# Strassen-like second layer of a fused attention and channel-mixer kernel: seven products summed in held PSUM banks for groups 1 to 5

## The chip, the cores and the metric

The kernel runs on one core of a Trainium2 chip. The metric is the device time of one execution in microseconds; lower is better. The engines are named as in the profile: PE (TensorE matmuls), PEld (TensorE weight loads), DVE (VectorE), ACT (ScalarE), POOL (GpSimd) and SP (SyncE, which issues DMAs).

## The reference

Causal attention with a bias from a running sum of `max(s, 0)`, on 8 batches of 8 heads, 576 positions, 64 dimensions; its output, as 8 x 576 tokens of 512 features, goes through a low-rank mixer over the positions and then a two-layer mixer over the features:

```
bias = -(cum[:, :, :, None] - cum[:, :, None, :])          # cum = cumsum(max(s, 0))
scores = where(causal, -1e9, q @ k.T / 8 + minimum(bias, 0))
x = softmax(scores) @ v                                    # to (8, 576, 512)
u = x + (x.transpose(0, 2, 1) @ U @ V).transpose(0, 2, 1)  # rank 32
out = u + maximum(u @ w_ch1, 0) @ w_ch2                    # 512 -> 2048 -> 512
```

## The kernel before

**Attention.** Work goes by pairs of heads, 32 in all (`n`). `scores` (L428) writes two-bank PSUM tiles `pscore` and one small tail in a one-bank tile `pwork`; ScalarE's exponential (L446, L458, L464) makes `pT`, and VectorE masks it (L372). `values` (L492) multiplies `pT` with `v` in two halves; VectorE takes a reciprocal (L501) and a product (L502) from each. Copies into `slot` (L362) bring the next pair's transposed q and k. `seqmix` is the low-rank mixer of a batch: products L522, L535, L567 and L592, VectorE copies L531 and L537, and evacuations into `uT` (L547) that add the transposed x.

**Feature mixer.** The 4608 tokens are cut into nine groups of 512 (`g`, NG = 9). `chanmix(g)` is a generator: 16 steps make `hT`, the hidden layer (L662, evacuated at L1044), then `outputs_by_quarters` does the second layer. It multiplies by Winograd's form of Strassen's scheme: `hT` and `w_ch2` are cut into quarters (A11 and so on, B11 and so on), and seven products of sums of quarters replace eight. The sums of A are VectorE's (`total`, L698, halves of 128x1024 each): A_1 = A21 + A22, A_2 = A_1 - A11, A_3 = A11 - A21 (written over A21) and A_4 = A12 - A_2. Each product (`product`, L720) has two halves of eight 128x256 matmuls and fills one PSUM bank. Adds (L734) make the four output quarters `o_sb` (three buffers), with `add_u` adding `u_sd`, the token-ordered u; `send` issues the output DMA on SP (L744).

In groups 1 to 5 each product takes a fresh `pwork` bank from a pool of four, which scores' tails, values, seqmix and the hidden layer use too. ScalarE copies the first product to `U2` (L843), and VectorE adds the others onto `U2` and the quarters. Groups 6 to 8 (`g >= NG - 3`) run mostly after the attention; there one bank `y` holds P1 while P6, P5 and P3 are added in the bank, and a second, `z`, takes the other products.

**Order.** Group 0's mixer and groups 1 to 6 are woven into the attention: `step_fill` runs one step of the front generator in `fill` at the share that `pace` gives for each attention step. PE's and POOL's order is that of the program text as traced. From batch 1 on a scheduler orders VectorE, ScalarE and SP by its own estimates, except where `placed` pins an instruction behind the VectorE instruction traced just before it. A weight's or an operand's wait therefore stops all of PE's later work. Bank slots are handed out by the scheduler from those that are free.

Of the kernel before, what the change touches and what calls it, by code (L numbers as in the profile page):

```python
# [12 lines left out]
FP32 = mybir.dt.float32  # L13
# [3 lines left out]
ALU = mybir.AluOpType  # L17
# [24 lines left out]
def kernel(  # L42
# [12 lines left out]
    nc = tc.nc  # L55
# [13 lines left out]
    NG = B * S // 512  # L69
# [170 lines left out]
    HF, HD = NF // 2, DM // 2  # L240
# [3 lines left out]
    B_3 = B12  # L244
# [448 lines left out]
    A_2 = half_sums(slots[4], "p a b -> p (a b)")  # L693
    A_4 = half_sums(v_slots[0], "p a b c -> p (a b c)")

    def total(dst, a, b, op, k4):
        at = (slice(None), slice(4 * k4, 4 * k4 + 4))
        nc.vector.tensor_tensor(dst[at], a[at], b[at], op=op)  # L698

    def first_sums(hT, one):  # L700
        if one:
# [4 lines left out]
    def outputs_by_quarters(g, hT, u_sd):  # L706
        A11, A12 = hT[:, :HF, :256], hT[:, HF:, :256]
        A21, A22 = hT[:, :HF, 256:], hT[:, HF:, 256:]
        A_3 = A21

        def bank(tag="y"):
            if g < NG - 3:
                tile = pwork()
            else:
                tile = ps_tail[0].tile([128, 512], FP32, tag=tag, name="quarter", bufs=1)
            return tile.rearrange("p (i d) -> p i d", i=2)

        def product(acc, a, b, i, begin=True):
            for kt in range(HF):
                nc.tensor.matmul(  # L720
                    acc[:, i, :],
                    lhsT=a[:, kt, ds(i * 128, 128)],
                    rhs=b[:, kt, :],
                    start=(begin and i == 0 and kt == 0),
                    stop=(kt == HF - 1),
                    skip_group_check=True,
                )

        def quarter():
            o = work.tile([128, DM], FP32, tag="o_sb", name="o_sb", bufs=3)  # L730
            return o.rearrange("p (i d) -> p i d", i=2)

        def add(dst, a, b):
            nc.vector.tensor_tensor(dst, a, b, op=ALU.add)  # L734
# [15 lines left out]

        halves = range(2)
        if g >= NG - 3:
            y = bank("y")
            for i in halves:
                product(y, A11, B11, i)
                total(*((A_1, A21, A22, ALU.add), (A_2, A_1, A11, ALU.subtract))[i], 1)
                yield
            o11 = quarter()
            add_u(o11, y, 0, 0)
            x = bank("z")  # L760
            for i in halves:
                product(x, A12, B21, i)
                total(A_3, A11, A21, ALU.subtract, i)
                yield
            add(o11, o11, x)
            send(o11, 0, 0)
            for i in halves:
                product(y, A_2, B_2, i, False)
                total(A_4, A12, A_2, ALU.subtract, i)
                yield  # L770
            o21 = quarter()
            add_u(o21, y, 1, 0)
            w = bank("z")
            product(w, A_3, B_3, 0)
            yield
            for i in halves:
                product(y, A_1, B_1, i, False)
                yield
            o22 = quarter()
            add_u(o22, y, 1, 1)  # L780
            product(w, A_3, B_3, 1)
            yield
            add(o22, o22, w)
            send(o22, 1, 1)
            if g == NG - 1:
                add(o21, o21, w)
                for c, i, lo, hi in (
                    (1, 0, 0, HD),
                    (0, 0, 0, HD),
                    (1, 1, 0, HD),  # L790
                    (0, 1, 0, 128),
                    (0, 1, 128, HD),
                ):
                    if c == 1:
                        product(y, A_4, B22, i, False)
                        if i == 0:
                            o12 = quarter()
                        add(
                            o12[:, i, :].rearrange("p (a b) -> p a b", a=2),
                            y[:, i, :].rearrange("p (a b) -> p a b", a=2),  # L800
                            u_sd[:, 2:4, i, :],
                        )
                        nc.sync.dma_start(
                            out=out_flat[ds(g * 512 + i * 128, 128), HD:], in_=o12[:, i, :]
                        )
                        continue
                    p4 = ps_t.tile([128, 512], FP32, tag="t", name="parts").rearrange(
                        "p (i d) -> p i d", i=2
                    )
                    for kt in range(HF):  # L810
                        nc.tensor.matmul(
                            p4[:, 0, lo:hi],
                            lhsT=A22[:, kt, ds(i * 128, 128)],
                            rhs=B_4[:, kt, lo:hi],
                            start=(kt == 0),
                            stop=(kt == HF - 1),
                        )
                    add(o21[:, i, lo:hi], o21[:, i, lo:hi], p4[:, 0, lo:hi])
                    (nc.sync if lo == 128 else nc.scalar).dma_start(
                        out=out_flat[ds(g * 512 + 256 + i * 128, 128), lo:hi],  # L820
                        in_=o21[:, i, lo:hi],
                    )
                return
            for i in halves:
                product(y, A_4, B22, i, False)
                yield
            o12 = quarter()
            add_u(o12, y, 0, 1)
            send(o12, 0, 1)
            for i in halves:  # L830
                product(w, A22, B_4, i, False)
                yield
            add(o21, o21, w)
            send(o21, 1, 0)
            yield
            return
        U2 = work.tile([128, 2, HD], FP32, tag="U2", name="U2", bufs=1)
        p1 = bank()
        for i in halves:
            product(p1, A11, B11, i)  # L840
            total(*((A_1, A21, A22, ALU.add), (A_2, A_1, A11, ALU.subtract))[i], 1)
            yield
        nc.scalar.copy(U2, p1)  # L843
        p2 = bank()
        for i in halves:
            product(p2, A12, B21, i)
            yield
        o = quarter()
# [17 lines left out]
        p3 = bank()  # L866
        for i in halves:
            product(p3, A_4, B22, i)
            if i == 0:
                o12 = quarter()  # L870
                add_u(o12, o22, 0, 1)
                total(A_3, A11, A21, ALU.subtract, 1)
            yield
        add(o12, o12, p3)
        send(o12, 0, 1)
        p7 = bank()
        for i in halves:
            product(p7, A_3, B_3, i)
            if i == 0:
                add_u(o22, o22, 1, 1)  # L880
            yield
        add(U2, U2, p7)
        add(o22, o22, p7)
        send(o22, 1, 1)
        p4 = bank()
        for i in halves:
            product(p4, A22, B_4, i)
            if i == 0:
                o21 = quarter()
                add_u(o21, U2, 1, 0)  # L890
                yield
        add(o21, o21, p4)
# [461 lines left out]
```

## Time and profile before

| | |
|---|---|
| median of 3 runs | 347.36 us (347.32 to 347.95) |
| profiled execution | 347.92 us, of which the span is 346.1 us |
| granted clock | 0.999 |
| instructions | 8930 |
| second layers of groups 1 to 5, from first to last matmul | within 94 to 113, 132 to 150, 170 to 189, 208 to 226 and 247 to 265 us |
| end of the attention with its mixing | about 281 us |

A timeline row gives the start and length of merged instructions, engine, line, operation, operands, count, and in brackets the engine's idle time before it with what ended it. A group's row gives least, median and greatest nanoseconds of one instruction.

### The profile page before, as it was taken

How to read it: one execution, taken by the hardware profiler on the slowest of the kernel's cores; microseconds unless marked ns; L12 is line 12 of the kernel's file. 1: busy time of each engine (PE TensorE's matmuls, PEld its weight loads, DVE VectorE, ACT ScalarE, POOL GpSimd, SP SyncE). 2: the span in 40 equal slices, each digit the busy share in tenths (PEclk: the TensorE clock that was granted, in tenths of full speed). 3: DMA queues.
4: the chain of work that ended last, by engine and by line, in shares of the span. 5: the costliest groups of instructions: out<-in, count | busy, mean ns of one | idle time of the engine just before them, and what ended most of it. 6: DMA issues, size and time to landing. Idle time of an engine off the chain costs nothing.

```text
span 346.1 us, 8930 instructions
## 1 busy us (share of the span) xinstructions
PE 336.4 (97%) x3607; PEld 243.7 (70%) x3641; DVE 260.6 (75%) x576; ACT 203.9 (59%) x308; POOL 125.8 (36%) x183
## 2 busy tenths in 40 slices
PE   8999999999999999999999999999999999999996
PEld 4685556656688558865678568865687568888885
DVE  8894756778799668974898469965988597875874
ACT  4786985638850886178624883388552546665710
POOL 7997358848494309431823374000000000000000
PEclk9999999999999999999999999999999999999999
DMA  7999999999999999999999999495025252010022
GB/s 107 154 180 207 182 185 127 160 204 204 148 167 168 203 138 102 134 196 152 117 117 176 176 128 149 109 179 68 14 56 136 57 95 59 30 63 32 30 93 91
DMA packets 169696, 44.09 MB, mean 127 GB/s; under 512 B 154584, under 2 KB 168024, under 8 KB 169656
## 3 DMA queue, kind: packets, MB, share of 16 engines
q0 software_dynamic: 99440, 18.44, 71.0%
q1 hardware_dynamic: 69928, 24.90, 38.5%
q8 instruction: 28, 0.46, 0.6%
q10 hardware_dynamic: 288, 0.20, 0.2%
q14 instruction: 12, 0.10, 0.1%
HBM read 37.25 MB, written 9.70 MB: 136 GB/s over the span
## 4 chain that ended last, share of the span: by engine, by line
PE 81%; DVE 10%; ACT 4%; issue 3%; DMA 1%; SPq 0%; DVEq 0%; ACTq 0%
PE pwork L662 23%; PE pwork L720 13%; PE quarter L720 10%; PE pscore L428 10%; PE pwork L492 8%; PE parts L952 6%; PE pwork L681 3%; DVE uT L547 2%; DVE slot L698 1%; DVE o_sb L734 1%; DMA slot<-hT 1%; PE pwork L952 1%; PE pscore L662 1%; ACT hT L1044 1%; PE pwork L522 1%
## 5 line engine op out<-in xcount | busy, mean ns | idle before, releaser
L662 PE MATMUL pwork<-uT,w_sb 128*128 128x512 bf16 x407 | 104.2, 379 | 1.9 <-ACT pT L464 0.5
L1044 ACT ACTIVATE hT<-pwork 128x512 bf16<-128x512 f32 x107 | 64.8, 610 | 37.5 <-PE pwork L662 36.6
L446 ACT ACTIVATE pT<-pscore 128x1024 bf16<-128x1024 f32 x57 | 57.5, 1031 | 49.7 <-PE pscore L428 49.4
L662 PEld LDWEIGHTS <-w_sb 128*128 128x128 bf16 x448 | 39.2, 98 | 38.8 <-issue 1.0
L121 POOL DMA_DIRECT2D qk_sd<-in_q_dram x46 | 34.3, 746 | 71.8 <-DMA qk_sd<-qk_sd 34.6
L428 PE MATMUL pscore<-slot 68*128 68x128 bf16 (+1 forms) x506 | 55.8, 245 | 0.8 <-DMA slot<-hT 0.6
L428 PEld LDWEIGHTS <-slot 68*128 68x128 bf16 x570 | 42.2, 97 | 18.5 <-DMA slot<-hT 0.8
L720 PEld LDWEIGHTS <-hT 128*128 128x128 bf16 x496 | 46.7, 98 | 7.2 <-DVE uT L547 0.5
L372 DVE TENSOR_TENSOR pT<-pT,keep 128x512 bf16<-128x512 bf16 (+1 forms) x81 | 28.7, 355 | 27.7 <-ACT pT L446 21.0
L492 PEld LDWEIGHTS <-pT 128*128 128x128 bf16 x870 | 32.5, 97 | 6.2 <-issue 0.9
L178 POOL DMA_DIRECT2D v_slot<-in_v_dram x40 | 34.0, 862 | 5.7 <-DMA w_sb<-in_moe_w_ch_dram 5.2
L492 PE MATMUL pwork<-v_slot,pT 128*128 128x65 bf16 x870 | 35.4, 193 | 0.2 <-DVE uT L547 0.2
L121 POOL DMA_DIRECT2D qk_sd<-in_k_dram x46 | 33.7, 733 | 1.5 <-DMA v_slot<-in_v_dram 1.3
L502 DVE TENSOR_TENSOR x_sb<-pwork,rec 128x320 bf16<-128x320 f32 x64 | 31.2, 489 | 1.4
L458 ACT ACTIVATE pT<-pscore 128x1024 bf16<-128x1024 f32 x29 | 30.3, 1046 | 2.7 <-PE pscore L428 2.6
L720 PE MATMUL pwork<-w_sb,hT 128*128 128x256 bf16 x240 | 29.9, 273 | 0.0
L720 PEld LDWEIGHTS <-slot 128*128 128x128 bf16 x256 | 24.1, 98 | 4.1 <-issue 1.1
L335 DVE COPY slot<-pwork 64x576 bf16<-64x576 bf16 x27 | 21.7, 803 | 3.5 <-PE pwork L316 1.8
L501 DVE RECIPROCAL rec<-pwork 128x5 f32<-128x5 f32 x64 | 12.1, 190 | 12.1 <-PE pwork L492 11.4
L720 PE MATMUL pwork<-w_sum,slot 128*128 128x256 bf16 x160 | 20.1, 273 | 0.3 <-DVE o_sb L734 0.3
L720 PE MATMUL quarter<-w_sb,hT 128*128 128x256 bf16 x144 | 18.0, 273 | 0.3 <-DVE uT L547 0.3
L362 DVE COPY slot<-qk_sd 64x1152 bf16<-64x1152 bf16 x30 | 16.3, 542 | 0.3
(164 smaller groups left out, 486.9 us busy)
## 6 DMA issues: line engine op xcount, KB each, us to landing
out_dram<-o_sb SPq DMA_DIRECT2D x34, 256.0 KB
v_slot<-in_v_dram POOLq DMA_DIRECT2D x32, 128.0 KB, 6.4
w_sb<-in_moe_w_ch_dram POOLq DMA_DIRECT2D x4, 1024.0 KB, 13.3
qk_sd<-in_q_dram POOLq DMA_DIRECT2D x46, 72.0 KB, 4.4
qk_sd<-in_k_dram POOLq DMA_DIRECT2D x46, 72.0 KB, 4.6
qk_sd<-in_q_dram POOLq DMA_DIRECT2D x5, 144.0 KB, 5.1
qk_sd<-in_k_dram POOLq DMA_DIRECT2D x5, 144.0 KB, 5.2
qk_sd<-in_q_dram POOLq DMA_DIRECT2D x2, 288.0 KB, 9.1
```

The lines of the kernel that those rows point to most:

```text
L121: nc.gpsimd.dma_start(out=of_pair(n)[:, c, :, hh, :], in_=src[b, 2 * hp + hh].rearrange("(t p) d -> p t d", p=TR),)
L178: nc.gpsimd.dma_start(out=vt[:rows_t, t, :, 0:D], in_=v[b, :, ds(t * 128, rows_t), :].rearrange("h p d -> p h d"),)
L372: nc.vector.tensor_tensor(dst, dst, keep[:, :, 0:w].to_broadcast([128, n_tiles, w]), op=ALU.min)
L428: nc.tensor.matmul(dst, lhsT=slot[0:KA, hh, ds(S + j * 128, 128)], rhs=slot[0:KA, hh, lo:hi], start=True, stop=True,)
L446: nc.scalar.activation(pT[:, hh, 0:1024], near, EXP, scale=scale)
L458: nc.scalar.activation(pT[:, :, 1024:1536], mid.rearrange("p (a b) -> p a b", a=2), EXP, scale=scale)
L492: nc.tensor.matmul(po[:, i, :], lhsT=pT[:, hh, ds(place(j, i), 128)], rhs=vt[:, j, h, :], start=(j == 0), stop=(j == i), skip_group_check= ...
L502: nc.vector.tensor_tensor(x_sb[:, hp, :, ds(hh * D, D)], po[:, :, 0:D], rec.to_broadcast([128, 5, D]), op=ALU.mult,)
L662: nc.tensor.matmul(f1, lhsT=w1_sb[:, kt, ds(nf * 128, 128)], rhs=u[:, kt, :], start=(kt == 0), stop=(kt == 3),)
L720: nc.tensor.matmul(acc[:, i, :], lhsT=a[:, kt, ds(i * 128, 128)], rhs=b[:, kt, :], start=(begin and i == 0 and kt == 0), stop=(kt == HF - ...
L952: nc.tensor.matmul(acc[:, i, :], lhsT=w[:, kt, ds((2 * e + i) * 128, 128)], rhs=m[:, kt, :], start=(begin and i == 0 and kt == 0), stop=(k ...
L1044: nc.scalar.activation(hT[:, nf, :], f1, RELU)
```

## The change

Groups 1 to 5 now run the same sequence of products and adds as groups 6 to 8: `y` collects P1, P6, P5 and P3 in one bank, `x` and then `w` hold the other products, `w` collecting P7 and P4. Their banks still come from the pool of four (`pwork`). `U2`, its ScalarE copy and the adds onto it are gone. In these groups the halves of A_3 are summed beside the A_2 products and those of A_4 beside the A_1 products, each through `placed`; in groups 6 to 8 they stay where they were. A group of 1 to 5 has 15 steps in place of 14. The lines of groups 6 to 8 are only moved out of an `if`.

```
-    def total(dst, a, b, op, k4):
+    def total(dst, a, b, op, k4, pinned=False):
         at = (slice(None), slice(4 * k4, 4 * k4 + 4))
-        nc.vector.tensor_tensor(dst[at], a[at], b[at], op=op)
+
+        def ins():
+            nc.vector.tensor_tensor(dst[at], a[at], b[at], op=op)
+
+        placed(ins) if pinned else ins()
...
-            if g < NG - 3:
+            if not tail:
                 tile = pwork()
...
+        halves, tail = range(2), g >= NG - 3
+        y = bank("y")
+        for i in halves:
+            product(y, A11, B11, i)
+            total(*((A_1, A21, A22, ALU.add), (A_2, A_1, A11, ALU.subtract))[i], 1)
+            yield
+        o11 = quarter()
+        add_u(o11, y, 0, 0)
+        x = bank("z")
+        for i in halves:
+            product(x, A12, B21, i)
+            if tail:
                 total(A_3, A11, A21, ALU.subtract, i)
+            yield
+        add(o11, o11, x)
+        send(o11, 0, 0)
+        for i in halves:
+            product(y, A_2, B_2, i, False)
+            if tail:
                 total(A_4, A12, A_2, ALU.subtract, i)
+            else:
+                total(A_3, A11, A21, ALU.subtract, i, True)
+            yield
+        o21 = quarter()
+        add_u(o21, y, 1, 0)
+        w = bank("z")
+        product(w, A_3, B_3, 0)
+        yield
+        for i in halves:
+            product(y, A_1, B_1, i, False)
+            if not tail:
+                total(A_4, A12, A_2, ALU.subtract, i, True)
+            yield
+        o22 = quarter()
+        add_u(o22, y, 1, 1)
+        product(w, A_3, B_3, 1)
+        yield
+        add(o22, o22, w)
+        send(o22, 1, 1)
...
         for i in halves:
+            product(y, A_4, B22, i, False)
+            yield
+        o12 = quarter()
+        add_u(o12, y, 0, 1)
+        send(o12, 0, 1)
         for i in halves:
+            product(w, A22, B_4, i, False)
+            yield
+        add(o21, o21, w)
         send(o21, 1, 0)
         yield
...
-        U2 = work.tile([128, 2, HD], FP32, tag="U2", name="U2", bufs=1)
-        p1 = bank()
-        for i in halves:
-            product(p1, A11, B11, i)
-            total(*((A_1, A21, A22, ALU.add), (A_2, A_1, A11, ALU.subtract))[i], 1)
-            yield
-        nc.scalar.copy(U2, p1)
-        p2 = bank()
...
-        add_u(o, U2, 0, 0)
-        add(o, o, p2)
-        send(o, 0, 0)
-        p6 = bank()
-        for i in halves:
-            product(p6, A_2, B_2, i)
-            if i == 1:
-                total(A_4, A12, A_2, ALU.subtract, 0)
-            yield
-        add(U2, U2, p6)
-        p5 = bank()
-        for i in halves:
-            product(p5, A_1, B_1, i)
-            total(*((A_4, A12, A_2), (A_3, A11, A21))[i], ALU.subtract, 1 - i)
-            yield
-        o22 = quarter()
-        add(o22, U2, p5)
...
```

More of the change, by code (lines that the diff above doesn't have):

```diff
@@ L749, in send @@
             )
-        halves = range(2)
-        if g >= NG - 3:
-            y = bank("y")
-            for i in halves:
-                product(y, A11, B11, i)
-                total(*((A_1, A21, A22, ALU.add), (A_2, A_1, A11, ALU.subtract))[i], 1)
-                yield
-            o11 = quarter()
-            add_u(o11, y, 0, 0)
-            x = bank("z")
-            for i in halves:
-                product(x, A12, B21, i)
-                total(A_3, A11, A21, ALU.subtract, i)
-                yield
-            add(o11, o11, x)
-            send(o11, 0, 0)
-            for i in halves:
-                product(y, A_2, B_2, i, False)
-                total(A_4, A12, A_2, ALU.subtract, i)
-                yield
[L771 to L778, printed above, removed]
-            o22 = quarter()
[L780 to L836, printed above, removed]
@@ L837, in outputs_by_quarters @@
-        U2 = work.tile([128, 2, HD], FP32, tag="U2", name="U2", bufs=1)
-        p1 = bank()
+        halves, tail = range(2), g >= NG - 3
+        y = bank("y")
         for i in halves:
-            product(p1, A11, B11, i)
+            product(y, A11, B11, i)
             total(*((A_1, A21, A22, ALU.add), (A_2, A_1, A11, ALU.subtract))[i], 1)
             yield
-        nc.scalar.copy(U2, p1)
-        p2 = bank()
+        o11 = quarter()
+        add_u(o11, y, 0, 0)
+        x = bank("z")
         for i in halves:
-            product(p2, A12, B21, i)
+            product(x, A12, B21, i)
+            if tail:
+                total(A_3, A11, A21, ALU.subtract, i)
@@ L847, in outputs_by_quarters @@
             yield
-        o = quarter()
-        add_u(o, U2, 0, 0)
-        add(o, o, p2)
-        send(o, 0, 0)
-        p6 = bank()
-        for i in halves:
-            product(p6, A_2, B_2, i)
-            if i == 1:
-                total(A_4, A12, A_2, ALU.subtract, 0)
-            yield
-        add(U2, U2, p6)
-        p5 = bank()
+        add(o11, o11, x)
+        send(o11, 0, 0)
+        for i in halves:
+            product(y, A_2, B_2, i, False)
+            if tail:
+                total(A_4, A12, A_2, ALU.subtract, i)
+            else:
+                total(A_3, A11, A21, ALU.subtract, i, True)
+            yield
@@ new lines, in outputs_by_quarters @@
+        product(w, A_3, B_3, 1)
+        yield
+        add(o22, o22, w)
+        send(o22, 1, 1)
+        if g == NG - 1:
+            add(o21, o21, w)
+            for c, i, lo, hi in (
+                (1, 0, 0, HD),
+                (0, 0, 0, HD),
+                (1, 1, 0, HD),
+                (0, 1, 0, 128),
+                (0, 1, 128, HD),
+            ):
+                if c == 1:
+                    product(y, A_4, B22, i, False)
+                    if i == 0:
+                        o12 = quarter()
+                    add(
+                        o12[:, i, :].rearrange("p (a b) -> p a b", a=2),
+                        y[:, i, :].rearrange("p (a b) -> p a b", a=2),
+                        u_sd[:, 2:4, i, :],
+                    )
+                    nc.sync.dma_start(
+                        out=out_flat[ds(g * 512 + i * 128, 128), HD:], in_=o12[:, i, :]
+                    )
+                    continue
+                p4 = ps_t.tile([128, 512], FP32, tag="t", name="parts").rearrange(
+                    "p (i d) -> p i d", i=2
+                )
+                for kt in range(HF):
+                    nc.tensor.matmul(
+                        p4[:, 0, lo:hi],
+                        lhsT=A22[:, kt, ds(i * 128, 128)],
+                        rhs=B_4[:, kt, lo:hi],
+                        start=(kt == 0),
+                        stop=(kt == HF - 1),
+                    )
+                add(o21[:, i, lo:hi], o21[:, i, lo:hi], p4[:, 0, lo:hi])
+                (nc.sync if lo == 128 else nc.scalar).dma_start(
+                    out=out_flat[ds(g * 512 + 256 + i * 128, 128), lo:hi],
+                    in_=o21[:, i, lo:hi],
+                )
+            return
@@ L873, in outputs_by_quarters @@
+        for i in halves:
+            product(y, A_4, B22, i, False)
             yield
-        add(o12, o12, p3)
+        o12 = quarter()
+        add_u(o12, y, 0, 1)
         send(o12, 0, 1)
-        p7 = bank()
         for i in halves:
-            product(p7, A_3, B_3, i)
-            if i == 0:
-                add_u(o22, o22, 1, 1)
+            product(w, A22, B_4, i, False)
             yield
[L882 to L892, printed above, removed]
+        add(o21, o21, w)
         send(o21, 1, 0)
```

6 lines of the change are left out of this document (removed).

## The prediction

> **What bounds the kernel now.** First the page, for the balance of the engines over the span:
>
> ```profile
> PE 336.4 (97%) x3607; PEld 243.7 (70%) x3641; DVE 260.6 (75%) x576; ACT 203.9 (59%) x308; POOL 125.8 (36%) x183
> ```
>
> TensorE is the bound, and the change leaves its matmuls as they are in number and shape. It can act only through TensorE's waits. How many are there now where the change acts? The windows view, cut at the second layers of groups 1 to 5 (columns: stretch, length, busy time and count of PE, PEld, DVE, ACT, POOL, clock, DMA share, GB/s):
>
> ```profile
> 90.00:115.00 25.00, 24.60 (x289) 19.39 (x289) 23.62 (x53) 11.55 (x18) 15.39 (x21) 1.00 1.69 166
> 140.00:151.00 11.00, 10.95 (x136) 9.47 (x136) 10.90 (x24) 3.07 (x4) 3.80 (x5) 1.00 1.37 149
> 176.00:189.00 13.00, 12.44 (x163) 10.75 (x162) 11.37 (x26) 3.24 (x4) 3.78 (x5) 1.00 1.75 123
> 209.00:227.00 18.00, 17.95 (x220) 15.54 (x219) 17.66 (x41) 7.32 (x11) 2.95 (x4) 1.00 1.17 128
> 247.00:265.00 18.00, 17.95 (x227) 15.79 (x227) 15.42 (x37) 7.14 (x10) 0.00 (x0) 1.00 0.26 59
> ```
>
> PE is idle for 0.40 + 0.05 + 0.56 + 0.05 + 0.05 = 1.1 us in all of these. VectorE is 86 to 99% busy there, but PE hardly ever waits for it: today each product goes to a fresh bank, and ScalarE's copy and VectorE's adds run behind. The adds, from the view of L734:
>
> ```profile
> L734 DVE TENSOR_TENSOR o_sb<-U,u_sd x10: 680/686/693, 98.2 to 264.0; 128x512 f32<-128x512 f32 x10
> L734 DVE TENSOR_TENSOR o_sb<-quarter,u_sd x4: 687/692/698, 283.7 to 302.3; 128x512 f32<-128x512 f32 x4
> ```
>
> The second row is the same add read straight from a held bank, as group 6 does it: 0.69 us either way. Last the timeline of group 1's second layer, for the order of the waits:
>
> ```profile
> 97.61 0.69 DVE L698 TENSOR_TENSOR hT<-hT 128x1024 bf16<-128x1024 bf16 x1
> 98.21 0.69 DVE L734 TENSOR_TENSOR o_sb<-U,u_sd 128x512 f32<-128x512 f32 x1
> ...
> 100.88 1.94 ACT L446 ACTIVATE pT<-pscore 128x1024 bf16<-128x1024 f32 x2 [3.89 <-PE pscore L428]
> ...
> 101.12 1.04 PE L720 MATMUL pwork<-w_sum,slot 128*128 128x256 bf16 x8
> ...
> 102.70 0.84 PEld L720 LDWEIGHTS <-slot 128*128 128x128 bf16 x8
> ...
> 103.81 0.39 PE L567 MATMUL pscore<-V_sb,ux 32*128 32x512 bf16 x2
> ...
> 104.41 1.28 DVE L547 TENSOR_TENSOR uT<-pscore,xT 128x768 bf16<-128x768 f32 x2
> 105.60 0.75 DVE L547 TENSOR_TENSOR uT<-pwork,xT 128x384 bf16<-128x384 f32 x2
> ```
>
> The first two rows give VectorE's pace: an add lasts 0.69 us, but the next starts 0.60 us after it. Matmuls of 128x256 follow each other every 0.109 us (8 in 0.87).
>
> **What goes.** Per group VectorE loses four adds (eleven L734 adds and ScalarE's L843 copy today, seven adds after): 20 x 0.60 = 12 us of its queue, and 5 x 0.58 us of ScalarE's. Both are off the path. The gain is at most the 1.1 us that PE idles there, and no wait of L720 for L734 but one of 0.3 us stands among PE's waits, so I take 0. The cover is PE's own work.
>
> **What comes: PE now waits for VectorE.** Bank `y` takes P1, then P6, P5 and P3 on top, and each next product must wait until the add has read the one before. The halves of A_3 and A_4 are pinned behind the VectorE instruction traced just ahead of them, and come one or two products later than today; a product needs the second half at its fifth matmul, 0.44 us after its start. I go through the built program's order with the durations above, group by group.
>
> Group 1, A_3. The second half of A_3 will stand behind the second score mask (L372, 0.42 us, the next starts after 0.33). That mask waits for the second of the two exponentials, which ends at 100.88 + 1.94 = 102.82. The add of `y` into o21 goes ahead of it (ready at 101.12 + 1.04 = 102.16, its 0.60 over by 102.8). So the mask starts at 102.85, A_3 at 103.2, and its sum is there at 103.9. PE starts the A_3 product at 102.70, the row of the LDWEIGHTS, and stands at its fifth matmul at 103.14: 0.75 us. Behind PE's wait queue a score tail, the L567 products and the rest of the layer; nothing overtakes.
>
> Group 1, A_4. Between L567 and the A_4 product PE has 24 matmuls and four small ones: 2.6 + 0.1 = 2.7 us. VectorE must meanwhile do, in this order, the pair's evacuation (1.2), half of A_4 (0.6), two evacuations (0.67), the other half (0.6), two evacuations (0.67) and the add of `y` into o22 (0.69), on which the A_4 product waits: 4.4 us. It starts 0.2 us before PE leaves L567: 1.5 us. Today's waits there (0.1 on an add, 0.2 around L567) fall away: 1.95 for the group.
>
> Group 2. After L567 PE has 16 matmuls of A_2 (1.75) and four of A_3 (0.44) and then needs A_3's second half: 2.2 us. VectorE has the pair (1.2), half of A_3 (0.6), two evacuations (0.67) and the other half (0.69): 3.2, so 1.0 us. From there PE has four matmuls and L592 (0.55) until A_1's product, VectorE two evacuations (0.6) and the add into o21 (0.69): 0.7. Sum 1.7.
>
> Group 3. From the add of P1 on, VectorE has that add and half of A_3 (1.2), reciprocal, its result's wait and product (0.64) and the other half (0.69): 2.5. PE has two halves of values (0.9), eight matmuls and four (1.3): 2.2, so 0.3; and another 0.3 in the same way for the add into o21. Today's waits there (L592 0.21, L720 for L734 0.30) lose their place. Net 0.1.
>
> Group 4. Two exponentials back to back again, ending at 218.03 + 1.94 = 219.97 by today's rows; mask and half of A_3 bring 221.0. PE is at the fifth matmul at 220.0 (217.38 for the first score, then 12 scores, eight matmuls, four scores, four matmuls). 1.05, and 0.3 for one read of `y`: 1.35. Group 5, no mixing beside it, as group 3: 0.5.
>
> **The step that is moved.** A group has 15 steps, the last without a matmul, against 14. Five filler steps of group 6 thus move behind the attention. There they stand between the last mixing's products, where PE today waits for evacuations (L592 and the first `quarter` product, 0.4 and 0.5 us around 280 us): -0.8. POOL's queue is not touched; SP's four sends a group stay four, each behind its own add, and nobody waits for them but the o_sb buffer of two quarters later.
>
> **Held banks.** Two of four banks are held through a layer, which no layer of the trace does with attention beside it. A bank fewer can't gain, so the lower bound is 0. Upper bound: one late bank per half of the values, each until reciprocal and product are done (0.10 + 0.49), four a group: 5 x 4 x 0.6 = 12 us. I take 0.5, near the lower end, since the order gives a freed bank a full product's time (0.87) before it is wanted again, more than the 0.6.
>
> Sum: 1.95 + 1.7 + 0.1 + 1.35 + 0.5 - 0.8 + 0.5 = +5.3 us.
>
> The Trainium skill's page "Perfetto Trace Analysis", section "Optimizing Tensor Performance", says that independent groups of matmuls should rotate through different PSUM banks, so that the evacuation of one overlaps the next group's matmuls. It speaks against this change: by it alone, with each of the 15 reuses of `y` bare for one add of 0.69 us, the sum would be +10.4. The rows of today's rotation, 0.3 us of waits for adds, agree with it as far as they go.
>
> The profiled execution took 347.92 us: 346.1 of span and 1.8 around it. The runs' median is 347.36, 0.56 lower. 347.92 + 5.3 = 353.2 for such an execution, and 352.7 for a median.
>
> **The rivals.**
>
> Faster. VectorE is 94 to 99% busy in three of the windows; 12 us less in its queue lets every evacuation come sooner, and the A sums too. If these run ahead of PE, today's waits vanish (1.1 us) and those at 280 us as well (0.8): 347.36 - 1.9 = 345.5. It decides where the add of `y` ends before PE's next product, as it does in group 1's first reuse (two halves of values and a product of 16 matmuls, 2.9 us, lie between). Against it: the second exponential, not VectorE's load, sets A_3 in groups 1 and 4. Chance 0.08.
>
> No difference: the waits come but only as small as in group 3, 0.3 us at a place, some 2 us in all, and the 1.1 and 0.8 us pay for them: 347.4. Against it: group 1's A_4 has 4.4 us of queue for 2.7 of cover. Chance 0.03.
>
> Small loss: the masks' exponentials come earlier than today in groups 1 and 4 since ScalarE lost its copy, halving those waits, and the held banks cost nothing: 348.1 to 350.3. Chance 0.11.
>
> Banks. The upper bound above adds up: 12 us in place of 0.5 gives 364; half of it, 358. What speaks for it is seqmix, which needs two banks at once; against it, the banks' readers end 0.6 us after PE. Chance 0.08.
>
> That the change does not do what it says: the order shows 20 L734 adds and five copies fewer and the same matmuls, so I give it nothing.
>
> **How the numbers follow.** My forecast, waits of 3 to 8.5 us: 350.4 to 355.9, 352.7 likeliest, chance 0.70. The range 348.8 to 356.2 holds it and most of the small loss. This kernel's runs tell a difference of about 0.2% (0.7 us). Slower 0.70 + 0.11 + 0.08 = 0.89, the same 0.03, faster 0.08.
>
> **What would show it.** Right: PE waits on A_3's in-place sums (hT) and on adds into o_sb from `pwork`, some 6 us together, the largest 1 to 2 us in group 1 around 103 and 109 us, others in groups 2 and 4; VectorE some 12 us less busy; each second layer's window with 0.5 to 2.5 us of PE idle. Wrong: PE idle near 1 us in these windows, or its waits on L501, L502 or L547 for a bank, or a changed wait after the attention.

## The result and the profile after

| | before | after |
|---|---|---|
| median of 6 runs each | 347.94 us | 353.99 us |
| lowest to highest | 347.32 to 349.07 us | 353.75 to 354.07 us |
| profiled execution, its span | 347.92 us, 346.1 us | 353.75 us, 352.1 us |

The ratio is 1.0169, 95% interval 1.0150 to 1.0188: slower by 6.05 us. The forecast was 352.7 us in a range of 348.8 to 356.2 us. Before's median is 347.94 us here, 347.36 in the runs that the forecast started from, and 347.53 to 347.72 in the comparisons below; measured against those, the loss would be 6.3 to 6.5 us. A difference between after and a kernel below is thus uncertain by some 0.4 us.

Below, *excess* means a kernel's median minus the median of the kernel before in the same comparison; after's is +6.05 us. In the traces of after the lines are shifted: `product` is L724, the adds L738, the sums of A L700, the hidden layer's evacuation L994.

The balance of the engines first, from the page of after:

```profile
PE 337.7 (96%) x3608; PEld 243.0 (69%) x3641; DVE 251.5 (71%) x557; ACT 200.5 (57%) x302; POOL 126.1 (36%) x183
```

VectorE lost 9.1 us of work and ScalarE 3.4, and the span grew by 6.0. PE's work is the same: 3641 weight loads, and a `product` matmul's record still lasts 273 ns on average. (The 1.3 us that PE's busy time grew lie in modelled ends.) So the time can only be waiting. The windows of after, cut as before:

```profile
90.00:115.00 25.00, 22.73 (x275) 18.14 (x273) 20.25 (x47) 8.81 (x13) 15.63 (x21) 1.00 1.77 165
140.00:151.00 11.00, 9.71 (x111) 7.64 (x110) 9.84 (x22) 1.12 (x3) 3.78 (x5) 1.00 1.58 106
176.00:189.00 13.00, 12.50 (x155) 10.50 (x153) 11.87 (x27) 3.74 (x6) 3.78 (x5) 1.00 1.49 130
209.00:227.00 18.00, 16.98 (x199) 13.38 (x198) 16.24 (x38) 6.75 (x11) 5.62 (x7) 1.00 1.28 118
247.00:265.00 18.00, 17.82 (x214) 13.32 (x214) 13.44 (x32) 9.72 (x15) 0.00 (x0) 1.00 0.19 43
```

PE is idle for 2.27 + 1.29 + 0.50 + 1.02 + 0.18 = 5.3 us, against 1.1 us before, and VectorE is no fuller than it was. The stretches stand at before's times, and two of them leave out the start of a layer; the layers of after stand up to 7 us later. Cut at each kernel's own layers, PE is idle for 5.4 us in after and 1.2 us in before. PE's waits of after say for whom it waits:

```profile
PE pwork L724 <- DVE hT L700: 2.6, 4, 0.9
PE pwork L724 <- DVE o_sb L738: 2.5, 4, 1.4
```

Both are VectorE instructions in front of a product: the sums of A, and the adds that read `y`. The timeline of group 1's second layer shows one of each (in brackets PE's idle time ahead of the row):

```profile
100.64 1.94 ACT L446 ACTIVATE pT<-pscore 128x1024 bf16<-128x1024 f32 x2 [4.48 <-PE pscore L428]
...
102.64 0.42 DVE L372 TENSOR_TENSOR pT<-pT,keep 128x512 bf16<-128x512 bf16 x1
102.97 0.68 DVE L700 TENSOR_TENSOR hT<-hT 128x1024 bf16<-128x1024 bf16 x1
...
103.72 0.61 PE L724 MATMUL pwork<-w_sb,hT 128*128 128x256 bf16 x4 [0.86 <-DVE hT L700]
...
108.60 0.68 DVE L738 TENSOR_TENSOR o_sb<-pwork,u_sd 128x512 f32<-128x512 f32 x1
...
109.34 1.03 PE L724 MATMUL pwork<-w_sb,v_slot 128*128 128x256 bf16 x8 [1.37 <-DVE o_sb L738]
```

The exponentials end at 102.58, the mask starts at 102.64 behind them, and the second half of A_3 at 102.97 behind the mask. PE stands until it is there. At 108.60 the add reads `y`, at the end of a queue of evacuations and both halves of A_4; PE stands until it has ended. The adds themselves have their old length, as L738's view shows:

```profile
L738 DVE TENSOR_TENSOR o_sb<-pwork,u_sd x20: 651/684/692, 96.3 to 268.7; 128x512 f32<-128x512 f32 x20
L738 DVE TENSOR_TENSOR o_sb<-o_sb,pwork x15: 669/687/690, 99.0 to 270.5; 128x512 f32<-128x512 f32 x15
```

They are no dearer, only fewer, and now PE waits for some of them.

### The profile page after: what moved, and what is told of

Same layout as the page of the kernel before. It is cut to its first block, busy times and chain, and to the rows that moved or that the text cites. A ratio compares the mean times of both kernels' runs of the same rounds, so it can differ in the third digit from the quotient of the medians.

```text
span 352.1 us, 8908 instructions
## 1 busy us (share of the span) xinstructions
PE 337.7 (96%) x3608; PEld 243.0 (69%) x3641; DVE 251.5 (71%) x557; ACT 200.5 (57%) x302; POOL 126.1 (36%) x183
## 4 chain that ended last, share of the span: by engine, by line
PE 75%; DVE 13%; ACT 5%; issue 3%; DMA 2%; POOL 1%; SPq 0%; DVEq 0%; ACTq 0%
PE pwork L662 22%; PE pwork L724 13%; PE pscore L428 9%; PE quarter L724 8%; PE pwork L492 8%; PE parts L902 6%; PE pwork L681 3%; DVE o_sb L738 2%; DVE uT L547 2%; DMA v_slot<-in_v_dram 2%; ACT pT L446 2%; DVE hT L700 2%; DVE slot L700 1%; PE pscore L662 1%; PE pwork L522 1%
## 5 line engine op out<-in xcount | busy, mean ns | idle before, releaser
L994 ACT ACTIVATE hT<-pwork 128x512 bf16<-128x512 f32 x106 | 64.0, 609 | 40.1 <-PE pwork L662 37.7
L724 PEld LDWEIGHTS <-hT 128*128 128x128 bf16 x496 | 46.5, 98 | 11.1 <-DVE hT L700 4.4
L724 PE MATMUL pwork<-w_sb,hT 128*128 128x256 bf16 x240 | 31.4, 273 | 2.8 <-DVE hT L700 2.6
L724 PEld LDWEIGHTS <-slot 128*128 128x128 bf16 x256 | 24.1, 98 | 6.0 <-issue 2.9
L724 PE MATMUL pwork<-w_sum,slot 128*128 128x256 bf16 x160 | 20.3, 272 | 0.9 <-DVE o_sb L738 0.8
L724 PE MATMUL quarter<-w_sb,hT 128*128 128x256 bf16 x144 | 18.0, 272 | 0.2 <-ACT hT L994 0.2
L738 DVE TENSOR_TENSOR o_sb<-pwork,u_sd 128x512 f32<-128x512 f32 x20 | 13.7, 685 | 4.1 <-PE pwork L724 3.8
```

Source lines behind the costliest of these rows:

```text
L724: nc.tensor.matmul(acc[:, i, :], lhsT=a[:, kt, ds(i * 128, 128)], rhs=b[:, kt, :], start=(begin and i == 0 and kt == 0), stop=(kt == HF - ...
L994: nc.scalar.activation(hT[:, nf, :], f1, RELU)
```

## The experiments

The theory: the late, fixed sums of A and the reads of `y` between products each make PE wait, and what VectorE saves was hidden before. The rivals: held banks starve the rest of PE's work; or VectorE's load, or the moved step, decides.

### The sums as in groups 6 to 8

A_3 is summed beside A12*B21 and A_4 beside the A_2 products, one product earlier, and neither is fixed.

```
         product(x, A12, B21, i)
-            if tail:
-                total(A_3, A11, A21, ALU.subtract, i)
+            total(A_3, A11, A21, ALU.subtract, i)
...
         product(y, A_2, B_2, i, False)
-            if tail:
-                total(A_4, A12, A_2, ALU.subtract, i)
-            else:
-                total(A_3, A11, A21, ALU.subtract, i, True)
+            total(A_4, A12, A_2, ALU.subtract, i)
...
-            if not tail:
-                total(A_4, A12, A_2, ALU.subtract, i, True)
```

> The changed kernel, with the sums of A_3 beside the A12*B21 products and those of A_4 beside the A_2 products in groups 1 to 5 as in groups 6 to 8, and not pinned. Theory of the two waits: the 2.6 us that PE waits for A_3's sums (hT) go, and the 2.5 us of waits for the reads of y shrink, since in group 1 the halves of A_4 (2 x 0.6 us) no longer stand before the read on which PE waits 1.4 us: 350 to 351 us. Rival, held banks: two of four banks are held as before, so 354 within 0.7. Rival, steps and order: 15 steps as before, so 354.

Measured: 350.27 us, ratio 1.0091 (1.0058 to 1.0124), excess +2.74. The waits for hT are gone, those for `o_sb` fell from 2.5 to 1.0 us. As the theory had it. But compare the next two kernels, which leave the sums where they are.

### Both sums in their late places, but not fixed

```
-                total(A_3, A11, A21, ALU.subtract, i, True)
+                total(A_3, A11, A21, ALU.subtract, i)
...
-                total(A_4, A12, A_2, ALU.subtract, i, True)
+                total(A_4, A12, A_2, ALU.subtract, i)
```

> The changed kernel, its halves of A_3 and A_4 asked for at the same places but without being fixed there: the planner then sets them ahead of the second mask and of most evacuations. Theory 1 (the late sums cost most of the loss: they stand behind a mask that waits for an exponential, or among evacuations): PE's waits of 2.6 us on hT go, and the add into o21 or o22 that reads y in group 1 has 1.2 us less ahead of it, so its waits of 2.5 us shrink to about 1; 348.7 to 350.3 us. Theory 2 (holding y and reading it between products is what costs, wherever the sums stand): 352 us or more, with the waits on o_sb at 2.5 us or above.

Measured: 348.69 us, ratio 1.0035 (1.0022 to 1.0049), excess +0.97. Two arguments out of the code take 5.1 of the 6.05 us away. PE's waits of this kernel and its products at the same places in group 1:

```profile
PE pwork L724 <- DVE o_sb L738: 1.0, 4, 0.4
```

```profile
102.20 1.04 PE L724 MATMUL pwork<-w_sb,hT 128*128 128x256 bf16 x8
...
107.09 1.03 PE L724 MATMUL pwork<-w_sb,v_slot 128*128 128x256 bf16 x8 [0.17 <-DVE o_sb L738]
```

The A_3 product runs its eight matmuls in one go, and the wait for `y` is 0.17 us in place of 1.37. The kernel with the earlier sums is 1.6 us slower, but not in the layers: from the first to the last L522 the two profiled executions take 204.5 (earlier sums) and 204.1 us, while that first L522 stands at 67.4 against 65.6 us, ahead of the change. In the profiled execution this is the clock: between 13 and 18 us it was granted at 0.79 and 0.57 of full speed, and the same four matmuls take longer, first in the kernel with the earlier sums, then in this one:

```profile
15.68 1.89 PE L205 MATMUL pwork<-busy 128*128 128x512 bf16 x4
```

```profile
14.62 1.03 PE L205 MATMUL pwork<-busy 128*128 128x512 bf16 x4
```

But nine of that kernel's twelve runs had a mean clock of 1.000 and still took 349.9 to 351.0 us. They have no trace, so what makes the medians differ is open.

### Only A_3 freed

A_4's argument stays.

```
-                total(A_3, A11, A21, ALU.subtract, i, True)
+                total(A_3, A11, A21, ALU.subtract, i)
```

> The changed kernel with A_3's halves free, as in the run before, and A_4's halves fixed at their late places. This parts the two sums. Theory 1a (A_3's wait behind the mask and A_4's load on the read of y are two separate prices, 2.6 us on hT and 2.5 us on o_sb): the first goes, the second stays, 351.4 us (350.8 to 352). Theory 1b (the fixed A_4 alone is the harm): 353.3 or more. Theory 1c (A_3 alone is the harm): 350 or less.

Measured: 349.76 us, ratio 1.0061 (1.0049 to 1.0073), excess +2.04: the time that was expected if A_3 alone does the harm. But it is not A_3 alone: freeing A_3 gives 6.05 - 2.04 = 4.0 us, and freeing A_4 as well gives 2.04 - 0.97 = 1.1 us more. The first is more than the 2.6 us that PE's waits name. The weight loads say why, in their group on the page of after (busy time, mean ns, idle time ahead with its releaser):

```profile
L724 PEld LDWEIGHTS <-hT 128*128 128x128 bf16 x496 | 46.5, 98 | 11.1 <-DVE hT L700 4.4
```

4.4 us of their idle time ends with a sum. The matmuls' records, whose ends are modelled, cover part of it. PE's waits with A_3 freed, and the read of `y` in group 1:

```profile
PE pwork L724 <- DVE o_sb L738: 2.4, 4, 1.4
```

```profile
108.29 1.03 PE L724 MATMUL pwork<-w_sb,v_slot 128*128 128x256 bf16 x8 [1.37 <-DVE o_sb L738]
```

So the sums' prices are separate. The 1.37 us of group 1 stay as long as A_4's halves stand among the evacuations, and are 0.17 without them: most of them belong to A_4's place, not to `y` alone.

### ScalarE reads `y`

ScalarE copies `y` into U2 (one copy for three of the reads), VectorE adds from there; the sums are late and fixed as in the change.

```
+        def read(y):
+            if tail:
+                return y
+            U2 = work.tile([128, 2, HD], FP32, tag="U2", name="U2", bufs=1)
+            nc.scalar.copy(U2, y)
+            return U2
...
-        add_u(o11, y, 0, 0)
+        add_u(o11, read(y), 0, 0)
```

and so for o21 and o22.

> The changed kernel, but in groups 1 to 5 ScalarE copies bank y to SBUF (U2) before each of its first three reads and VectorE adds from the copy; the sums stay late and pinned. Theory of the two waits: y is free once ScalarE has read it, so the 2.5 us of PE waits for adds (o_sb) go; the 2.6 us for A_3's sums stay: 351 to 352 us, PE's waits for hT still there in groups 1, 2 and 4. Rival, held banks: 354 within 0.7, since y and w are held as before.

Measured: 350.85 us, ratio 1.0086 (1.0055 to 1.0117), excess +3.32. The wait on the add is gone, only that on the sums is left:

```profile
PE pwork L724 <- DVE hT L700: 2.8, 4, 0.9
```

The read of `y` was late because VectorE's queue was long, not because a bank was read: a free engine reads it at once. That is worth 6.05 - 3.32 = 2.7 us, about the 2.5 us of waits.

### Both remedies

The earlier sums and ScalarE's copy, both edits above on one kernel:

```
-            if tail:
-                total(A_3, A11, A21, ALU.subtract, i)
+            total(A_3, A11, A21, ALU.subtract, i)
...
-        add_u(o21, y, 1, 0)
+        add_u(o21, read(y), 1, 0)
```

> Both of the former edits at once: sums early and not pinned, and y copied by ScalarE. Theory of the two waits: 354.0 - 2.6 - 2.5 = 348.9 us, with PE waits on hT and o_sb under 0.5 us together; a little less if VectorE's lighter queue (20 adds fewer than before the change) helps. Rival, held banks: 354, as the banks y and w are held through each layer as before. Rival, that lighter queue is a gain: below 347.

Measured: 348.88 us, ratio 1.0031 (1.0003 to 1.0058), excess +1.35. No wait of a product is left among PE's waits, but two small ones take their place:

```profile
PE pwork L522 <- DVE x_sb L502: 0.5, 1, 0.5
PE pwork L567 <- ACT pT L464: 0.5, 1, 0.5
```

L567 does not read pT, so what it waits for can only be a bank: the exponential of a score tail has to read it empty first. The held banks are felt, at half a microsecond here.

### Fresh banks in the new order

The order of after and its late, fixed sums, but every product except the last in a fresh bank (P4 still goes on top of P7 in `w`), with U2, its copy and ten adds a group, where after has seven and before eleven.

```
+        if not tail:
+            nc.scalar.copy(U2, y)
...
+        y = y if tail else bank()
         for i in halves:
-            product(y, A_2, B_2, i, False)
+            product(y, A_2, B_2, i, not tail)
...
+        if not tail:
+            add(U2, U2, y)
```

and so for P5 and P3.

> The changed kernel's order of products and its late pinned sums in groups 1 to 5, but P1, P6, P5 and P3 each in a fresh bank, copied by ScalarE (P1) or added by VectorE onto U2 as before the change: ten adds and a copy, only w held. Theory of the two waits: the 2.5 us of waits for reads of y go, the 2.6 us for A_3's late sums stay, as in the kernel with the copied y (350.85): 350.5 to 352. Rival, held banks: one held bank fewer than there, so clearly below it, 349 or less.

Measured: 351.79 us, ratio 1.0118 (1.0103 to 1.0133), excess +4.25.

```profile
PE pwork L724 <- DVE hT L700: 3.3, 5, 1.0
PE pwork L724 <- DVE uT L547: 1.0, 1, 1.0
```

Rotation removes all waits for `y` and brings 6.05 - 4.25 = 1.8 us net: the waits for the sums are longer (3.3 for 2.6), presumably since three more adds a group stand in VectorE's queue, and one product now waits for an evacuation of unrelated data, so for a bank. The time is where the theory of the two waits had it: most of the loss does not come from holding `y`.

### Fresh banks and the earlier sums

The same banks and adds as in the last kernel, the sums as in groups 6 to 8:

```
-                total(A_3, A11, A21, ALU.subtract, i, True)
...
-                total(A_4, A12, A_2, ALU.subtract, i, True)
...
+            total(A_3, A11, A21, ALU.subtract, i)
...
+            total(A_4, A12, A_2, ALU.subtract, i)
```

> The same with the sums early and not pinned: order of products and 15 steps of the changed kernel, but neither late sums nor a held y. Theory of the two waits: 354.0 - 5.1 - nothing else = 348.9, and below it by what the held banks took in early_copy (PE waited 0.5 there for a bank, L567 for L464): 347 to 348.5, PE waits on hT and o_sb under 0.4. Rival, the order of products itself costs: 349 or more.

Measured: 349.71 us, ratio 1.0056 (1.0027 to 1.0086), excess +2.17; a miss. The granted clock differs between this kernel's runs: six at 0.998 or above took 347.4 to 349.1 us, six at 0.990 to 0.995 took 350.3 to 352.9. The former are about what was expected; why this kernel meets the lower clock so often is open. Even the former are no faster than before, so the new order of products by itself gains nothing. Nor are the early sums free: in the profiled execution (clock 1.000) L522 of group 1 waits 0.9 us for `x_sb`; VectorE takes half of A_4, at 98.98 us, ahead of the reciprocals and products that make it.

### The change without its last step

```
         send(o21, 1, 0)
-        yield
     return
```

> The changed kernel without the last, empty step of groups 1 to 5, so 14 steps as before the change. By the moved step (the kernel before gained 0.97 from a fifteenth step): 355.0 us. Rival, the step only shifts which attention step lies beside which product, and with it the waits for A_3 and y: anywhere from 353 to 356, with other waits than the changed kernel's in groups 3 and 5.

Measured: 354.10 us, ratio 1.0188 (1.0175 to 1.0201), excess +6.56, so 0.5 us above after's; the two ratios' intervals overlap. PEld's timeline of this kernel, then of before:

```profile
286.40 0.17 PEld L592 LDWEIGHTS <-ux 128*128 128x128 bf16 x4 [0.61 <-DVE uT L547]
...
287.39 1.64 PEld L724 LDWEIGHTS <-hT 128*128 128x128 bf16 x16 [0.55 <-DVE uT L547]
```

```profile
280.30 0.17 PEld L592 LDWEIGHTS <-ux 128*128 128x128 bf16 x4 [0.61 <-DVE uT L547]
...
281.29 1.64 PEld L720 LDWEIGHTS <-hT 128*128 128x128 bf16 x16 [0.54 <-DVE uT L547]
```

The two waits at the handover from the attention to group 6's second layer, absent in after, are back as they were. That part of the prediction's mechanism is shown. But it brings nothing: in their place after has two others, 0.42 us in front of the second load of group 6's first product and 0.32 us in front of a weight load of group 7's hidden layer (L902) at 292.52. The stretch from that layer's first load (280.40 in before, 286.50 here, 285.91 in after) to the second product's loads from `slot` takes 6.91 us here as in before, and 7.38 in after; the 0.47 are about what the wait of L592 just ahead of that stretch cost. PE's waits for hT and `o_sb` also differ (2.8 and 3.0 us, five each), since every filler step stands elsewhere, so the step's own price in the changed kernel is not settled to better than 0.1 (by the medians) to 0.7 us (by the ratios).

### The kernel before with the step

The step alone, added to the kernel before.

```
         send(o21, 1, 0)
         yield
+        yield
```

> The kernel before, with one more step without a matmul at the end of the second layer of groups 1 to 5 (15 steps in place of 14). By the prediction's moved step: five filler steps of group 6 go behind the attention and fill PE's waits around 280 us, -0.8: 347.1 us. Rival: an empty step leaves an attention step bare while PE waits for an exponential, +0.3 each: 348.5 or more.

Measured: 346.56 us, ratio 0.9964 (0.9944 to 0.9985), excess -0.97: faster than before. That is near the -0.8 of the prediction, but the gain does not come from the handover. There 0.42 us of waiting is left, in front of one product:

```profile
280.02 1.62 PEld L720 LDWEIGHTS <-hT 128*128 128x128 bf16 x15 [0.42 <-issue]
```

With 0.32 us more at 285.56, it takes back what the two old waits gave. By the starts of the weight loads 1.4 us are gained between 150 and 187 us, and 0.5 lost elsewhere. In that stretch the kernel before has waits that the one with the step has not, such as these:

```profile
168.46 0.55 PEld L662 LDWEIGHTS <-w_sb 128*128 128x128 bf16 x4 [0.55 <-DVE x_sb L502]
...
177.76 0.17 PEld L592 LDWEIGHTS <-ux 128*128 128x128 bf16 x4 [0.48 <-DVE uT L547]
```

With a step more per group another filler step lies beside each attention step. That such a shift falls out well here was not forecast.

### The kernel before with less on VectorE

The kernel before without its four `add_u` in each of groups 1 to 5 (u is left out of their outputs), twenty adds of 0.69 us in all. It removes as many adds as the change does, and leaves the order of the products as it is.

```
-        add_u(o, U2, 0, 0)
-        add(o, o, p2)
+        add(o, U2, p2)
...
-                add_u(o12, o22, 0, 1)
```

and so for the other two.

> The kernel before without its four adds of u per group in groups 1 to 5 (those groups' output lacks u): VectorE does 20 adds fewer, as many as the change takes away, and nothing else is moved by hand. By the prediction VectorE's load is off the path: 347.5 within 0.7. Rival, VectorE's load bounds these stages: their 1.1 us of PE idle go, 346.4 or less.

Measured: 346.35 us, ratio 0.9958 (0.9930 to 0.9986), excess -1.19. The expected 347.5 was missed, and the rival was right: twenty adds less on VectorE are worth 1.2 us. The windows show where; of group 1 and group 3:

```profile
90.00:115.00 25.00, 24.95 (x293) 19.75 (x294) 21.43 (x49) 12.16 (x19) 15.64 (x21) 1.00 1.87 159
...
176.00:189.00 13.00, 12.87 (x163) 10.82 (x163) 9.89 (x24) 3.97 (x6) 4.38 (x6) 1.00 1.42 187
```

PE's idle time there fell from 0.40 to 0.05 and from 0.56 to 0.13 us: it hung on VectorE's queue.

### One held bank

The kernel before with the step, and one `pwork` bank taken out of the rotation.

```
+        held = bank()
+        nc.tensor.matmul(
+            held[:, 0, 0:32], lhsT=A11[:, 0, 0:128], rhs=B11[:, 0, 0:32], start=True, stop=True
+        )
...
         send(o21, 1, 0)
+        nc.scalar.copy(U2[:, 0, 0:32], held[:, 0, 0:32])
```

> The kernel before with the further empty step in groups 1 to 5 (346.56 us), and with one of the four pwork banks held from the start to the end of each of their second layers: a matmul of 128x32 writes it at the start, ScalarE reads 128x32 of it at the end (five matmuls and five copies, about 0.1 us each, and nothing of the output depends on them). It measures the price of a held bank by itself. The prediction's term: +0.5 us for both held banks, so about 347.1 here. Rival (three banks are too few for products, halves of values and the pair of mixing at once; each late bank costs up to 0.6 us, four places a group): +3 to +6 us, 349.5 to 352.5, with PE's waits on L501, L502, L547 or the first matmul of a product for a bank.

Measured: 353.24 us, ratio 1.0157 (1.0144 to 1.0170), excess +5.52. Against the kernel with the step alone it is 5.52 + 0.97 = 6.5 us, more than the rival gave. PE's waits and one place of the timeline:

```profile
PE pwork L720 <- DVE uT L547: 1.6, 2, 0.8
...
PE pwork L720 <- ACT hT L1050: 0.8, 1, 0.8
PE pwork L720 <- ACT U L847: 0.7, 1, 0.7
```

```profile
105.36 0.74 DVE L547 TENSOR_TENSOR uT<-pwork,xT 128x384 bf16<-128x384 f32 x2
...
106.16 1.64 PEld L720 LDWEIGHTS <-v_slot 128*128 128x128 bf16 x16 [1.05 <-DVE uT L547]
```

The product at 106.16 reads nothing of uT; it waits 1.05 us until an evacuation has emptied its bank. By the starts of the weight loads, all that this kernel is slower than the one with the step alone (6.2 us between the two spans) lies inside the five layers, 0.6 to 1.8 us in each. The added matmuls and copies last 0.18 us each, ten in all. So with three banks for seven products, values and mixing, late readers of a bank come onto PE's path. The Trainium skill's page "Perfetto Trace Analysis", section "Optimization Strategy", says that the same gap repeating on the engine that should be saturated can mean too little room in PSUM for the next tile. This run agrees: with one bank fewer each layer loses time in gaps of 0.2 to 1.05 us, most of them in front of products.

### One bank for the last two products only

The kernel before with the step, in the order P1, P2, P6, P5, P7, P3, P4; P4 goes on top of P7 in its bank, which saves one add a group, and the A_3 sums come ahead of those of A_4.

```
-        p4 = bank()
+        p4 = p7
...
-            product(p4, A22, B_4, i)
+            product(p4, A22, B_4, i, False)
```

> The kernel before with the further empty step (346.56 us), the products in the order P1, P2, P6, P5, P7, P3, P4, and only P7 and P4 in one bank, P4 on top of P7, read into U2 and o22 in between as before is added late: nine adds and the copy in place of ten and the copy, A_3's sums ahead of A_4's, all in time. It holds one bank for the last four products of a layer instead of two through all of it. Theory (a bank held for a few products, with nothing read while it is held, costs nothing, and VectorE has five adds of 0.6 us less): 346.3 us (346.0 to 347.0). Rival (P4 must wait until P7's reader is done, and the bank is missed): 347.5 to 349.

Measured: 346.74 us, ratio 0.9972 (0.9960 to 0.9983), excess -0.98. That is inside the theory's range. It beats before and after, but not the kernel with the step alone (-0.97): neither the five saved adds nor the bank held across the last products show, or they cancel each other.

## Why the prediction was right, step by step

The waits were the ones forecast, and the time is within the range; three other terms were off, and partly cancel. PE's idle time, taken from the starts of the weight loads in both traces less the pace of their matmuls, and summed by stage (uncertain by some 0.2 us where a stage ends), against the terms:

| | forecast | after less before |
|---|---|---|
| group 1's layer | +1.95 | +2.2 |
| group 2's | +1.7 | +1.9 |
| group 3's | +0.1 | +0.3 |
| group 4's | +1.35 | +1.6 |
| group 5's | +0.5 | +0.7 |
| moved step, from the end of group 5's layer on | -0.8 | 0.0 |
| held banks, and all other stages | +0.5 | -0.6 |
| sum | +5.3 | +6.0 |

**The waits.** Group 1's two places were forecast at 0.75 and 1.5 us and show 0.86 and 1.37. The view of waits names the two kinds of releaser with 2.6 + 2.5 = 5.1 us, forecast "some 6". Each layer came out 0.2 to 0.25 us above its term. The order of the built program, walked through with durations of the old trace, was enough.

**Where the loss comes from.** The prediction put the reads of `y` and the late sums side by side. The runs part them: A_3's fixed place 4.0 us, A_4's 1.1, and 1.0 is left with both free. The reads of `y`, taken off VectorE, give 2.7 us, which overlaps with A_4's 1.1.

**What goes: mis-sized.** It was set at 0, with up to 1.1 us as the most. VectorE's busy time fell by 9.1 us, where 12 were forecast. Removing as many adds from the kernel before is worth 1.2 us. Of this the prediction had booked 0.8 as today's waits that fall away in groups 1 and 3, so the step's error is some 0.4 us, and toward a smaller loss.

**The moved step: mis-sized.** It was set at -0.8. The kernel without the step shows that it does remove the two waits that were named, but 0.42 and 0.32 us of new waiting take their place, and the handover comes out even. PE's waits in after name ScalarE's evacuation of the hidden layer, 0.2 us, for the first of them. The -0.97 of the kernel before with the step looks like the term, but was gained at 150 to 187 us: luck, not the mechanism. In the changed kernel the step is worth 0.1 to 0.7 us.

**Held banks: not seen, and with an argument that does not carry.** No wait for a bank stands among the larger PE waits of after; the kernel with both remedies shows one of 0.5 us, which is the term's size. But the prediction's reason, that a freed bank has a full product's time before it is wanted, fails in the kernel before: there one missing bank costs 6.5 us, over half of the 12 us that the prediction took as its upper bound for two. In after the products of a layer use the held banks themselves and leave the other two to the attention; this reading was not tested by a run of its own.

**All other stages** hold -0.6 us: -0.2 ahead of the first layer, where the two programs issue the same loads, and -0.3 between the layers (-0.7 between groups 2 and 3, +0.3 between 3 and 4), where the step shifts which filler lies beside which attention. So the sum's layers were 1.0 too low, the step 0.8 too good and the rest 1.1 too high. That these left 5.3 against 6.0 is in part luck.

**The rule on rotating banks.** The fresh banks are 1.8 us faster than the held ones with the sums late, and of the 15 reuses of `y` four made PE wait, 2.5 us in all. The rule of the Trainium skill's page "Perfetto Trace Analysis", section "Optimizing Tensor Performance", has its direction borne out by that; the +10.4 us that the prediction made of it are not. With the sums early, the fresh banks (349.71 us) are not clearly faster than the held ones (350.27, and 348.69 with the sums free).

**The rivals.** The faster rival needed sums ahead of PE. The kernel with the sums not fixed has just that, and is still at +0.97 in place of -1.9. Four reads of `y` still cost 1.0 us there, and the 0.8 at the handover was never to be had; the rest of the 2.9 us between the two is not parted. The rival with small losses assumed earlier exponentials; in group 1 they ended only 0.24 us earlier than in before (102.58 against 102.82), and all of after stands that much earlier there, from ahead of the change.

## What to carry to other kernels

Before an accumulation in a held bank saves adds, look at what is queued on the reading engine ahead of each read: while banks rotate nobody waits for that queue, and with a held bank TensorE does. An instruction that feeds TensorE should not be fixed behind one that waits for a third engine; here two such fixings cost 5.1 of 6.05 us, and leaving the place to the planner gave them back. A gain of the forecast size is no proof of its cause: look in the trace where it was gained. A bank counts by how many things want one in the same stretch: price it by a run that takes one away.

## What the runs showed of the hardware

The same program can run at a slightly lower mean granted clock on this one core. The trace of the kernel with the earlier sums (mean 0.995) shows where: the granted clock is 0.66 in the window from 13 to 18 us and 1.00 in the windows before and behind it. In that stretch four 128x512 matmuls in a row start about 0.42 us apart in place of 0.22, half the pace. By 0.66 of 5 us, some 1.7 us are lost (an estimate). In the kernel with fresh banks and earlier sums the six runs at 0.990 to 0.995 took about 1% longer than the others. The clock is not the whole of it: the kernel with the sums free has a run of 351.07 us, against 348.69 in the median, at 1.000.

VectorE's records overlap. The mask of group 1 lasts 0.42 us from 102.64 and the sum behind it starts at 102.97, 0.33 us later, so a queue is summed by starts, not by lengths. The Trainium skill's page "Perfetto Trace Analysis", section "Optimizing Scalar/DVE Operations", says that part of an instruction's profiled latency overlaps with the next instruction; these rows agree.
